# Splitting a weight load in four and reordering fillers and one AV in a fused attention and feed-forward kernel

## The chip, the cores and the metric

The kernel runs on one core of a Trainium2 chip. The metric is the device time of one execution in microseconds (us). One execution was also recorded by the hardware profiler; all times inside the execution are counted from the start of its recorded span. TensorE (PE) does the matmuls, VectorE (DVE) and ScalarE (ACT) do the elementwise work, GpSimd (POOL) does elementwise work and issues most loads, SyncE (SP) issues the rest.

## The reference

Eight batches of attention with 8 heads over 576 tokens, head size 64, are followed by a feed-forward layer over all 4608 tokens. The attention is a sum of two: one over tokens averaged by fours, whose result is repeated four times, and one in which each token sees only tokens less than four away.

```python
q_d = q.reshape(B, H, Sd, 4, D).mean(axis=3)       # k_d, v_d alike
out_up = np.repeat(sm_attn(q_d, k_d, v_d), 4, axis=2)
scores = np.where(abs(pos[:, None] - pos[None, :]) < 4, scale * q @ k.T, -1e9)
out_local = softmax(scores) @ v
x = (out_up + out_local).transpose(0, 2, 1, 3).reshape(B * S, H * D)   # 4608 x 512
h = x @ w_in                                       # 512 x 2048
out = (h * sigmoid(1.702 * h)) @ w_out             # 2048 x 512
```

## The kernel before

The order of the instructions on every engine is written out by hand (a manual schedule), so each engine executes its instructions in the order in which the code names them.

The feed-forward layer works in nine groups of 512 tokens. For one group, `mm1` (L706) multiplies 16 blocks of 128 columns of `w_in` with the transposed x (`hps_mm`, L690, matmul at L691, four steps of 128 over the 512 inputs) and `silu` (L701) writes each block to `gT`; `mm2` (L715, matmul at L747) multiplies `gT` with `w_out` into four tiles of 128 tokens, which ScalarE copies (L732) and SP stores (L737). Inside each group, at fixed positions, stand the steps of the attention of the next batch (`attention`, L648).

The first batch's attention stands ahead of all this, in its own order (L785 to L870), and it is there that the change is made. Its heads are taken in four pairs, hp 0 to 3. The steps are: the local scores (`scores`, L356, matmul at L367) and the averaged ones (`scores_d`, L378, matmul at L386); the exponentials on ScalarE (L397, L403); the averaged values by matmuls with a selection matrix (`prep_vd_pe`, L320, matmul at L329, copied by ScalarE at L338); then for each pair the local AV (`av_local0`, L500, matmul at L506) and the AV over averaged tokens, called the down AV here (`av_down0`, L514, matmuls at L520 and L529), both into one PSUM tile `o[hp]`. `normalise0` (L544) divides on VectorE: part "a" takes the columns of the local AV alone, part "b" the rest, each with a reciprocal (L548) and multiplications (L551, L556). `turned` (L848) transposes the normalised pair with matmuls (`transp_sum`, L564, matmuls at L571 and L582) and has ScalarE copy it into `xT` (`copy_x`, L590; L594 where the result lies in the two banks PM, L598 elsewhere). After the third and fourth pair, `part` (L843) starts the first group's L691 matmuls, as far as the finished pairs allow.

Between these steps stand fillers, `warm` (L641): matmuls of zeros at L644 into a PSUM bank, whose results are not read. `wz` holds zeros in bf16, `wf` in fp32. Without a named bank `warm` takes the next of the two banks PM in turn (`pm_tile`, L78).

The loads of w_in (`load_w_in`, L237), w_out (`load_w_out`, L246), k and q (`load_1`, L181) and, for the first two batches, v (`load_vb`, L214) are issued by POOL, in the order of the code. They turn fp32 in DRAM into bf16. POOL's loads use eight semaphores in turn, and each issue waits until the load eight places earlier has landed. `w_in_bf` is one tile; a matmul that reads some of its columns waits for the load that wrote those columns.

Of the kernel before, what the change touches and what calls it, by code (L numbers as in the profile page):

```python
# [19 lines left out]
def kernel(  # L20
# [48 lines left out]
    PM = [psum.tile([128, 512], FP32, name=f"pm{i}") for i in range(2)]  # L69
# [8 lines left out]
    def pm_tile():  # L78
        turn["m"] += 1
        return PM[turn["m"] % 2]  # L80

    wz = consts.tile([128, 512], BF16, name="wz")
    wf = consts.tile([128, 512], FP32, name="wf")
# [49 lines left out]
    def make_mask():  # L133
        nc.scalar.copy(
            out=mask.rearrange("p x (i c) -> p (x i) c", c=60),
            in_=dm[:, None, :].to_broadcast([128, 10, 60]),
        )
# [76 lines left out]
    def load_vb(b, i):  # L214
        for par in range(2):
            nc.gpsimd.dma_start(  # L216
                out=vbs[b % 2][64 * par : 64 * par + 64, i, :, 0:D],
                in_=bass.AP(
                    tensor=v.tensor,
                    offset=v[b, 0].offset + (114 * i + KSTART[par]) * D,  # L220
                    ap=[[D, 64], [S * D, H], [1, D]],
                ),
            )
# [13 lines left out]
    def load_w_in(c, n):  # L237
        nc.gpsimd.dma_start(
            out=w_in_bf[:, :, c : c + n],
            in_=bass.AP(  # L240
                tensor=moe_w_in.tensor, offset=moe_w_in.offset + c,
                ap=[[d_ff, 128], [128 * d_ff, n_dmc], [1, n]],
            ),
        )
# [133 lines left out]
    def scores_d(b, qd, sd=None):  # L378
        sd = sd or ps_tile()
        bank = banks(sd)  # L380
        for kc in range(3):
            for a in range(2):
                for r in range(4):
                    rows = slice(32 * r, 32 * r + 32)
                    j = r % 2
                    nc.tensor.matmul(  # L386
                        bank[r // 2][64 * j : 64 * j + 64, SD * kc : SD * kc + SD],
                        lhsT=kdT[qd][rows, 48 * kc : 48 * kc + 64, a],
                        rhs=qdT[b, qd][rows, :, a],
                        start=(a == 0), stop=(a == 1),  # L390
                        tile_position=(32 * r, 64 * j),
                    )
        return sd
# [8 lines left out]
    def exp_down(qd, sd):  # L402
        nc.scalar.activation(  # L403
            out=eds[qd][:, :, 0:432], in_=sd[:, :, 0:432],
            func=AF.Exp, scale=inv_sqrt_d / 16.0,
        )
# [107 lines left out]
    def av_down0(hp, o):  # L514
        Ed, vd, u = eds[hp // 2], vds[0], hp % 2
        h0 = hp - u
        for kc in range(3):
            for j in range(2):
                q0 = SD * kc + 128
                nc.tensor.matmul(  # L520
                    o[64:128, j, 260:390],
                    lhsT=Ed[64 * j : 64 * j + 48, u, q0 : q0 + 64],
                    rhs=vd[64 * j : 64 * j + 48, kc, h0 : h0 + 2, :],
                    start=(kc == 0), stop=(kc == 2),
                    tile_position=(64 * j, 64),
                )
        for kc in range(3):
            for j in range(2):
                nc.tensor.matmul(  # L529
                    o[:, j, 390:455],  # L530
                    lhsT=Ed[64 * j : 64 * j + 48, u, SD * kc : SD * kc + 128],
                    rhs=vd[64 * j : 64 * j + 48, kc, hp, :],
                    start=(kc == 0), stop=(kc == 2),
                    tile_position=(64 * j, 0),
                )
# [8 lines left out]
    def normalise0(o, y, u, parts="ab"):  # L544
        yl, yd, rc = y
        ov = o[:, :, 0:455].rearrange("p x (c e) -> p x c e", e=65)
        c0, c1 = {"a": (0, 4), "b": (4, 7), "ab": (0, 7)}[parts]
        nc.vector.reciprocal(rc[:, :, c0:c1], ov[:, :, c0:c1, 64:65])  # L548
        if "b" in parts:
            st = 2 - u  # L550
            nc.vector.tensor_tensor(  # L551
                out=yd.rearrange("p s x d -> p x s d"), in0=ov[:, :, 4 + u : 7 : st, 0:D],
                in1=rc[:, :, 4 + u : 7 : st].to_broadcast([128, 2, 2, D]), op=ALU.mult,
            )
            c1 = 6
        nc.vector.tensor_tensor(  # L556
            out=yl[:, :, c0:c1], in0=ov[:, :, c0:c1, 0:D],
            in1=rc[:, :, c0:c1].to_broadcast([128, 2, c1 - c0, D]), op=ALU.mult,
        )
# [4 lines left out]
    def transp_sum(y, x):  # L564
        y, yd = y[:2]
        for n, (slot, to, what) in enumerate((
            (1, x[0][:, 0:288], up(0, 72)),
            (1, x[1][:, 0:224], up(72, 128)),
            (0, x[1][:, 224:288], up(64, 80)),
        )):  # L570
            nc.tensor.matmul(  # L571
                to, lhsT=yd[:, slot, :, :], rhs=what,
                start=n < 2, stop=True, skip_group_check=True,
            )
        for m, par, pos0, n, c0, c1 in (
            (0, 0, 0, 2, 3, 60), (0, 0, 0, 1, 0, 3), (0, 1, 0, 2, 0, 57),
            (1, 0, 0, 1, 3, 60), (1, 0, 1, 1, 3, 60), (1, 1, 0, 2, 0, 57),
            (2, 0, 0, 1, 3, 60), (2, 1, 0, 1, 0, 60),
        ):
            t0 = 114 * (2 * m + pos0) + 60 * par + c0  # L580
            bank, t0 = t0 // 288, t0 % 288
            nc.tensor.matmul(  # L582
                sub(x[bank], t0, (114, n), (1, c1 - c0)),
                lhsT=y[:, par, 2 * m : 2 * m + 2, :],
                rhs=sub(id128, 64 * pos0 + c0, (64, n), (1, c1 - c0)),
                start=False, stop=True, skip_group_check=True,
            )
        return x

    def copy_x(b, hp, x):  # L590
        t0 = b * S
        if x is PM:
            for u in range(2):
                nc.scalar.copy(  # L594
                    out=xT[hp][:, t0 + 288 * u : t0 + 288 * u + 288], in_=x[u][:, 0:288]
                )
        else:
            nc.scalar.copy(  # L598
                out=xT[hp][:, t0 : t0 + S].rearrange("p (x t) -> p x t", x=2), in_=x,
            )  # L600
# [40 lines left out]
    def warm(n, cols=512, t=None, z=wz):  # L641
        t = pm_tile() if t is None else t
        for _ in range(n):
            nc.tensor.matmul(  # L644
                t[:, 0:cols], lhsT=z[:, 0:128], rhs=z[:, 0:cols], start=True, stop=True
            )
# [133 lines left out]
    o, y, x = {}, {}, {}  # L780
# [11 lines left out]
    for i in range(5):  # L792
        load_vb(0, i)
    for c in range(4):
        load_w_in(512 * c, 512)
    for qd in range(NQ):
        load_qk(1, qd)
# [19 lines left out]
    sp = scores(0, 1, barred=True, sp=PA[0:2])  # L817
    exp_local(1, sp)
    exp_down(0, scores_d(0, 0, PA[2]))
    warm(4)  # L820
    for hp in range(4):
        o[hp] = PA[hp % 3]
        y[hp] = y_tiles0()
# [9 lines left out]
        normalise0(o[hp], y[hp], hp % 2, "b")  # L833
    av_local0(2, o[2], range(5))
    normalise0(o[2], y[2], 0, "a")
    warm(2, t=PM[0], z=wf)
    make_mask()

    gT0 = new_gT()
# [8 lines left out]
    def turned(hp, n):  # L848
        x = PM if n is None else [PA[n][:, u, :] for u in range(2)]
        transp_sum(y[hp], x)  # L850
        copy_x(0, hp, PM if n is None else PA[n][:, :, 0:288])

    turned(0, None)
    av_down0(2, o[2])
    normalise0(o[2], y[2], 0, "b")
    turned(1, 1)
    av_local0(3, o[3], range(5))
# [87 lines left out]
```

## Time and profile before

| | us |
|---|---|
| median of 3 runs | 324.64 |
| lowest and highest run | 322.55, 325.23 |
| the profiled execution | 323.04 |
| its span, first to last instruction | 321.2 |
| PE busy | 312.3 (97% of the span) |
| ACT, POOL, DVE busy | 183.7, 139.3, 134.0 |

The mean granted TensorE clock of the profiled execution is 1.000. "Busy" counts the time in which an engine has at least one instruction in work. In the lists of instructions a row starts with its start and its length in us, then engine, source line and operation, then output and inputs with their shapes, the number of instructions, and in brackets the idle time ahead of it with what ended it ("issue" is idle time for which the profile shows no cause). Matmuls overlap, so the length of a group is somewhat more than the distance from its start to that of the next. PEld is TensorE's loading of weights.

### The profile page before, as it was taken

What the parts mean: (1) busy time and instruction counts of PE and PEld (TensorE: products, weight loads), DVE (VectorE), ACT (ScalarE), POOL (GpSimd) and SP (SyncE); (2) the same over time, 40 slices, a digit from 0 to 9 for tenths busy, and PEclk for the clock granted to TensorE, in tenths of its full rate; (3) what the DMA queues carried; (4) which work ended last, traced back from release to release, by engine and by line L of the source; (5) the groups of instructions that cost most, each with busy time, mean ns of one, the idle gap of its engine ahead of it and who ended that gap; (6) DMA issues with size and microseconds to landing.
All of it is one profiled execution on the core that took longest, in us unless ns stands there. A gap on an engine that the chain in (4) does not pass through costs nothing.

```text
span 321.2 us, 10997 instructions
## 1 busy us (share of the span) xinstructions
PE 312.3 (97%) x4927; PEld 157.6 (49%) x4927; DVE 134.0 (42%) x221; ACT 183.7 (57%) x314; POOL 139.3 (43%) x170
## 2 busy tenths in 40 slices
PE   6899999999999989999999999999999999999995
PEld 3565554445544445455545554555445544444444
DVE  6965326812773066605770478036811650000000
ACT  4465771767456663668365936583677466415611
POOL 8956950299009910794059604970296000000000
PEclk9999999999999999999999999999999999999999
DMA  7999999999519931796159815991360110020012
GB/s 121 128 206 207 170 149 216 183 248 209 132 68 198 201 97 67 168 215 147 66 147 205 177 40 147 200 203 49 109 106 2 70 67 2 0 98 33 2 62 68
DMA packets 64078, 40.02 MB, mean 125 GB/s; under 512 B 44064, under 2 KB 55456, under 8 KB 64032
## 3 DMA queue, kind: packets, MB, share of 16 engines
q1 hardware_dynamic: 44496, 24.32, 33.0%
q0 software_dynamic: 19392, 14.95, 31.9%
q8 instruction: 38, 0.62, 0.8%
q10 hardware_dynamic: 144, 0.07, 0.1%
q14 instruction: 8, 0.07, 0.1%
HBM read 44.83 MB, written 9.44 MB: 169 GB/s over the span
## 4 chain that ended last, share of the span: by engine, by line
PE 94%; DVE 2%; DMA 2%; issue 1%; POOL 0%; ACT 0%; POOLq 0%
PE pm L691 37%; PE pm L747 37%; PE pa L367 3%; PE pa L747 2%; PE pa L691 2%; PE pa L428 2%; PE pa L386 2%; PE pa L481 2%; DMA qb<-in_q_dram 2%; PE pa L450 2%; PE pm L762 1%; PE pm L644 1%; DVE qT L262 1%; PE pa L491 0%; PE pa L506 0%
## 5 line engine op out<-in xcount | busy, mean ns | idle before, releaser
L747 PE MATMUL pm<-w_out_bf,gT 128*128 128x512 bf16 x528 | 121.8, 380 | 0.3 <-issue 0.3
L691 PE MATMUL pm<-xT,w_in_bf 128*128 128x512 bf16 x544 | 121.1, 379 | 0.0
L702 ACT ACTIVATE gT<-pm 128x512 bf16<-128x512 f32 x136 | 81.0, 598 | 44.6 <-PE pm L691 44.6
L691 PEld LDWEIGHTS <-w_in_bf 128*128 128x128 bf16 x576 | 55.5, 98 | 66.9 <-issue 0.4
L747 PEld LDWEIGHTS <-gT 128*128 128x128 bf16 x560 | 51.4, 98 | 59.8 <-issue 1.0
L411 DVE TENSOR_TENSOR es<-es,mask 128x600 bf16<-128x600 bf16 x28 | 20.0, 730 | 88.8 <-ACT es L397 88.0
L292 POOL TENSOR_TENSOR pq<-kT 128x576 f32<-128x576 bf16 x14 | 16.2, 1159 | 90.0 <-DVE kT L262 90.0
L732 ACT ACTIVATE osb<-pm 128x512 f32<-128x512 f32 (+2 forms) x35 | 20.8, 594 | 40.4 <-PE pm L747 36.5
L605 ACT COPY od<-pa 128x384 f32<-128x384 f32 (+1 forms) x56 | 18.5, 412 | 32.2 <-DVE y L467 19.7
L467 DVE TENSOR_TENSOR y<-pa,rc 128x896 bf16<-128x896 f32 x28 | 30.6, 1092 | 1.0
L626 DVE TENSOR_TENSOR xT<-pa,od 128x570 bf16<-128x570 f32 x28 | 21.1, 753 | 11.4 <-ACT od L605 10.1
L734 DVE TENSOR_SCALAR osb<-pm 128x128 f32<-128x128 f32 x1 | 0.3, 292 | 55.3 <-ACT osb L732 55.3
L308 POOL TENSOR_TENSOR v<-v 112x512 f32<-112x512 f32 x18 | 22.8, 1266 | 0.0
L397 ACT ACTIVATE es<-pa 128x600 bf16<-128x600 f32 x32 | 19.7, 668 | 5.2 <-PE pa L367 5.0
L262 DVE STREAM_TRANSPOSE kT<-kb 128x576 f32<-128x576 f32 x16 | 20.0, 1249 | 3.5 <-DMA kb<-in_k_dram 3.4
L262 DVE STREAM_TRANSPOSE qT<-qb 128x576 f32<-128x576 f32 x16 | 19.9, 1241 | 0.4
L367 PEld LDWEIGHTS <-kT 32*64 32x64 bf16 x1280 | 11.7, 104 | 8.5 <-issue 6.4
L367 PE MATMUL pa<-qT,kT 32*64 32x60 bf16 x1280 | 13.6, 203 | 1.9 <-DVE qT L262 1.9
L216 POOL DMA_DIRECT2D vb<-in_v_dram x20 | 13.7, 698 | 3.0 <-DMA w_in_bf<-in_moe_w_in_dram 1.1
L292 POOL TENSOR_TENSOR pq<-qT 128x576 f32<-128x576 bf16 x13 | 14.9, 1146 | 0.0
L403 ACT ACTIVATE ed<-pa 128x864 bf16<-128x864 f32 x16 | 14.4, 898 | 0.1
L311 POOL TENSOR_TENSOR vd<-v 112x256 bf16<-112x256 f32 x18 | 13.7, 759 | 1.4
(92 smaller groups left out, 257.9 us busy)
## 6 DMA issues: line engine op xcount, KB each, us to landing
out_dram<-osb SPq DMA_DIRECT2D x35, 256.0 KB, 2.1
vf<-in_v_dram SPq DMA_DIRECT2D x60, 128.0 KB, 5.3
v<-in_v_dram SPq DMA_DIRECT2D x36, 192.0 KB, 5.1
kb<-in_k_dram POOLq DMA_DIRECT2D x16, 288.0 KB, 7.2
qb<-in_q_dram POOLq DMA_DIRECT2D x16, 288.0 KB, 8.3
w_in_bf<-in_moe_w_in_dram POOLq DMA_DIRECT2D x4, 512.0 KB, 9.1
w_out_bf<-in_moe_w_out_dram POOLq DMA_DIRECT2D x4, 512.0 KB, 12.6
vb<-in_v_dram POOLq DMA_DIRECT2D x20, 64.0 KB, 5.4
```

The source lines that it names most:

```text
L262: nc.vector.transpose(out=t32.rearrange("p (i c) -> p c i", c=18), in_=store[b, qd].bitcast(FP32).rearrange("p (c d) -> p c d", c=18),)
L292: nc.gpsimd.tensor_tensor(out=t1, in0=sv[:, :, 0:2, :], in1=sv[:, :, 2:4, :], op=ALU.add)
L308: eng.tensor_tensor(out=t1[0:112], in0=x[:, :, 0:2, :], in1=x[:, :, 2:4, :], op=ALU.add)
L367: nc.tensor.matmul(sp[r // 2][64 * par : 64 * par + 64, r % 2, 60 * i : 60 * i + 60], lhsT=kT[b, qd][rows, k0 : k0 + 64, a], rhs=qT[b, qd] ...
L397: nc.scalar.activation(out=es[2 * qd + u][:, :, 0:300], in_=sp[u][:, :, 0:300], func=AF.Exp, scale=inv_sqrt_d,)
L411: nc.vector.tensor_tensor(out=ev, in0=ev, in1=mask, op=ALU.mult)
L467: nc.vector.tensor_tensor(out=y[:, xs], in0=ov[:, :, :, 0:D], in1=rc[:, xs].to_broadcast([128, n, 7, D]), op=ALU.mult,)
L626: eng.tensor_tensor(out=sub(xT[hp], t0 + 3, (57, 2), (114, 5), (1, 57)), in0=sub(x, 3, (509, 2), (57, 5), (1, 57)), in1=sub(od, 3, (57, 2) ...
L691: nc.tensor.matmul(acc, lhsT=w_in_bf[:, dmc, ffc * 128 : (ffc + 1) * 128], rhs=xT[dmc][:, g * TG : g * TG + TG], start=(dmc == 0), stop=(d ...
L702: nc.scalar.activation(out=gT[:, ffc, :], in_=acc, func=AF.Silu, scale=GELU_SCALE)
L732: eng.activation(out=osb, in_=ap, func=AF.Copy, scale=1.0 / GELU_SCALE)
L747: nc.tensor.matmul(ops[t], lhsT=gT[:, ffc, t * 128 : (t + 1) * 128], rhs=w_out_bf[:, ffc, :], start=(ffc == 0), stop=(ffc == n_ffc - 1),)
```

## The change

Three places of the first batch's order change. The first 512 columns of w_in are loaded by four transfers of 128 columns each, in place of one of 512; the other three transfers of 512 follow as they did. The four bf16 fillers ahead of the averaged values become one fp32 filler into the bank PM[1], named instead of taken in turn, and of the two fp32 fillers behind the third pair's local AV one stays. The third pair's down AV is called ahead of the first `turned` instead of behind it; its normalisation "b" stays behind that `turned`.

```diff
@@ -792,6 +792,8 @@
     for i in range(5):
         load_vb(0, i)
     for c in range(4):
+        load_w_in(128 * c, 128)
+    for c in range(1, 4):
         load_w_in(512 * c, 512)
     for qd in range(NQ):
         load_qk(1, qd)
@@ -817,7 +819,7 @@
     sp = scores(0, 1, barred=True, sp=PA[0:2])
     exp_local(1, sp)
     exp_down(0, scores_d(0, 0, PA[2]))
-    warm(4)
+    warm(1, t=PM[1], z=wf)
     for hp in range(4):
         o[hp] = PA[hp % 3]
         y[hp] = y_tiles0()
@@ -833,7 +835,7 @@
         normalise0(o[hp], y[hp], hp % 2, "b")
     av_local0(2, o[2], range(5))
     normalise0(o[2], y[2], 0, "a")
-    warm(2, t=PM[0], z=wf)
+    warm(1, t=PM[0], z=wf)
     make_mask()
 
     gT0 = new_gT()
@@ -850,8 +852,8 @@
         transp_sum(y[hp], x)
         copy_x(0, hp, PM if n is None else PA[n][:, :, 0:288])
 
+    av_down0(2, o[2])
     turned(0, None)
-    av_down0(2, o[2])
     normalise0(o[2], y[2], 0, "b")
     turned(1, 1)
     av_local0(3, o[3], range(5))
```

## The prediction

> **What bounds the kernel.** I read the page's chain of work first, then TensorE's (PE) instructions in order of time from 13 to 30 us, where all three edits lie, then VectorE's (DVE) in the same stretch, and last the DMA issues with their times to landing.
>
> ```profile
> span 321.2 us, 10997 instructions
> ...
> PE   6899999999999989999999999999999999999995
> ...
> PE 94%; DVE 2%; DMA 2%; issue 1%; POOL 0%; ACT 0%; POOLq 0%
> ```
>
> TensorE carries 94% of the chain that ended last, and is full in nearly all slices. A microsecond is won only if TensorE gets to its dense matmuls (L691, L747) earlier, and nothing late stops it after that. The stretch that the change edits, in order of time (start, length, engine, line):
>
> ```profile
> 14.07 1.02 PE L644 MATMUL pm<-wz 128*128 128x512 bf16 x4 [0.31 <-issue]
> 15.03 0.83 PE L329 MATMUL pm<-vb,psel 128*64 128x256 bf16 x10
> ...
> 18.21 0.36 PE L520 MATMUL pa<-vd,ed 48*64 48x130 bf16 x6 [0.28 <-DVE yl L556]
> 18.50 0.27 PE L529 MATMUL pa<-vd,ed 48*128 48x65 bf16 x6
> 18.70 0.38 PE L506 MATMUL pa<-vb,es 64*64 64x65 bf16 x20
> 19.00 2.28 PE L644 MATMUL pm<-wf 128*128 128x512 f32 x4
> 21.12 0.41 PE L571 MATMUL pm<-id,yd 128*128 128x288 bf16 x3
> ...
> 21.75 0.36 PE L520 MATMUL pa<-vd,ed 48*64 48x130 bf16 x6
> ...
> 22.24 0.42 PE L571 MATMUL pa<-id,yd 128*128 128x288 bf16 x3
> ...
> 22.88 0.34 PE L506 MATMUL pa<-vb,es 64*64 64x65 bf16 x18
> ```
>
> The reader is to see that TensorE has no hole between 14 and 23 us longer than 0.31 us, but that the two L644 rows are fillers: their result is read by nobody. The two fp32 fillers (four passes, 19.00 to 21.12) cover a wait on VectorE:
>
> ```profile
> 19.86 0.20 DVE L548 RECIPROCAL rc<-pa 128x8 f32<-128x8 f32 x1
> 20.09 0.69 DVE L556 TENSOR_TENSOR yl<-pa,rc 128x512 bf16<-128x512 f32 x1
> ```
>
> This is the third pair's local normalisation. It reads the same accumulator that the pair's down AV (L520, L529) writes, and the order of instructions has that AV wait for VectorE. The price of such a release stands in the second pair: its L556 ran from 17.47 for 0.70 in the chain, to 18.17, and L520 started at 18.21, 0.04 later. The last two lines are landing times, in us after the issue: the first block of w_in (issued at 12.98) and the last block of the second batch's values (issued at 39.98).
>
> ```profile
> w_in_bf<-in_moe_w_in_dram POOLq DMA_DIRECT2D x1, 512.0 KB, 5.9
> vb<-in_v_dram POOLq DMA_DIRECT2D x1, 64.0 KB, 4.4
> ```
>
> **Part 1: four bf16 fillers become one fp32 filler.** Before, L329 starts 0.96 after the first bf16 filler (14.07 to 15.03). One fp32 filler is two passes. In the later pair of them the passes start at 19.00, 19.54, 20.27 and 20.70, and L571 follows at 21.12: so one filler takes 1.27 (19.00 to 20.27) or 0.85 (20.27 to 21.12). Against 0.96 that is -0.11 to +0.31. The 0.31 of issue ahead of the old filler may stay or go, so L329 could start up to 0.42 sooner or 0.31 later. Neither passes through whole: the last two of the first ten L329 loads sat idle 0.16 until 15.55 for the eighth value transfer (issued 10.71, landed 4.8 later, 15.51). Sooner gains at most 0.04; later loses 0.31 - 0.16 = 0.15. I take 0, as the two lengths lie 0.1 apart at the nearer row. Everything up to the local AV of the third pair (18.70) then stands where it was.
>
> **Parts 2 and 3: one of the two later fillers goes, and the third pair's down AV moves ahead of the first transposition.** They have one answer together. The local AV of pair 2 ends its starts at 19.00; one filler runs to 20.13 (second pass 19.54 + 0.59), at most 20.27. The next instruction is now the down AV's first matmul, which waits for the L556 that ends at 20.78. VectorE is not sped up by anything here: its work since 16.39 is released by the AVs ahead of the filler. So TensorE stands from 20.13 to 20.82 (20.78 + 0.04). Behind the waiting matmul stand, in TensorE's order, the first transposition (L571, L582), and with it ScalarE's copy of x (L594) that was 1.46 us idle anyway. From 20.82: down AV 0.49 (21.75 to 22.24), first transposition 0.63 (21.12 to 21.75), second 0.64 (22.24 to 22.88): 22.58. Before, the same point is 22.88. Gain 0.30. The same from the other side: 1.27 or 0.85 of filler leaves, and 0.69 of bare wait comes in its place. VectorE's end at 20.78 fixes this; I allow 0.1 either way for the start gaps.
>
> What comes next keeps its distance. Copies of x by ScalarE: the first transposition now ends near 22.0, the copy takes 0.70, and its first reader stands at 23.51 - 0.30 = 23.21. Pair 2's second normalisation starts about 21.35 instead of 22.35, and is needed near 23.4 instead of 23.74. Pair 3 moves as a whole. The filler names its PSUM bank instead of taking a turn, so the banks of all later tiles swap: mm2 of group 0 now first writes the bank that the last silu reads. That silu ends at 39.21 (38.61 + 0.60) and L747 starts at 39.66: 0.45 cover, and both move together. Cost 0; without the cover it would be the missing part of 0.45.
>
> **Part 4: w_in's first 512 columns in four transfers.** On TensorE nothing is won: the first block landed at 18.88 and its first reader started at 23.51. On POOL three more issues at 0.78 are 2.35 us. They delay the issues of the second batch's k and q, w_out and values; POOL idled for landings right after (1.03 and 2.34 ahead of w_out, 1.06 ahead of a value load), and up to there the queue holds several transfers, so the issue time itself costs 0. Each of those issues still waits for the transfer eight places earlier, which past the new ones is the same transfer as before.
>
> What can cost is the stream. The 512 packets of 1024 bytes become 2048 of 256. Rows of large packets moved 208 GB/s (18 to 20 us): 2.5 us for 512 KB. Rows of 128-byte packets moved 2135 packets in 2 us (10 to 12 us). At that packet rate 2048 packets take 1.9 us, a gain of 0.6; at that stretch's bytes (141 GB/s) 3.7 us, a loss of 1.2; at its worst stretch (96 GB/s, 12 to 14 us) 5.5 us, a loss of 2.9. 256 bytes lie nearer 128 than 1024, and a line through 0.94 ns a packet at 128 bytes and 4.9 at 1024 gives 1.5 ns, so 3.1 us: I take 0.6 later. Who meets it? The least cover is at the second batch's values: the last landed at 39.98 + 4.4 = 44.4, and L329 reads them at 46.49, or 46.19 after the gain: 1.8 us. w_out's first blocks landed at 35.8 and 38.35 for readers at 39.66 and 41.4; w_in's second at 22.0 for a reader past 26.7; the second batch's k and q, for which VectorE idles until 28.59, are read by TensorE at 38.50. SP's queue is not moved past: its first load waits for w_out's last block, at 50.45. A delay of 0.6 costs 0; 2.9 would cost 2.9 - 1.8 = 1.1.
>
> The Trainium skill speaks against this part: "DMA: Bandwidth & Descriptors", Specifications, wants at least 512 bytes a transfer, and says that below that the engine reads, modifies and writes. If that doubles the 2.5 us, the estimate by that page is 2.5 us later and 0.7 us lost, where the packet rows above make it nothing; the 128-byte rows here (141 GB/s against 208) do not show a doubling.
>
> **Sum.** 0 - 0.30 + 0 = -0.30; ends -0.44 (0.04 and 0.1 more gained) and +1.05 (-0.30 + 0.1 + 0.15 + 1.1). The profiled execution took 323.04 us (span 321.2), so 322.74. The median of the runs is 324.64, 1.60 above it, and the runs spread from 322.55 to 325.23; against the median I say 324.3.
>
> **Rivals.** *Nothing moves:* 0.3 us is given back at an issue gap downstream, as the 0.34 at L747 near 56.1 in the waits. For it: such gaps stand still while work moves. Against it: they need no common cause. 324.6.
>
> *The clock.* Less filler, and 0.69 of bare wait, could let TensorE slow down. The profile's granted clock is 1.00 throughout, but the first fillers (128x336) start 0.28 apart until about 5 us and 0.14 after, so half speed exists here, and left some 3.8 us after the first filler. Half speed for 3.8 us of the dense stretch costs 1.9. Against: TensorE stood 1.92 us with no matmul (6.74 to 8.66), and the ten fillers after that took 2.33, 0.22 a piece, full speed. It decides from a standstill of more than 1.9 us, or from too little work in the same few us. The price is 1.9 - 0.3 = 1.6: 326.2; two such stretches would be 328.1.
>
> The Trainium skill ("TensorE: Matmul & The Clock Gate", Why this matters for your kernels) allows idle gaps up to about 3 us. By it the clock holds and the sum stays; the 1.92 row agrees as far as it reaches.
>
> *The stream is late.* If w_in's pieces cost over 1.8 us, L329 at 46.49 stops for the values. At the worst row it ends at 324.64 - 0.3 + 1.1 = 325.4. This is slower than before, from one place.
>
> *More is won.* The runs' spread of 2.7 us means that some executions hold a wait which this profile doesn't show. If that is a late first block of w_in, four pieces give it back: up to the 1.6 between the median and the profiled execution, 324.64 - 0.3 - 1.6 = 322.7. Against it: 4.6 us of cover in the profile.
>
> **How the numbers follow.** Forecast 0.55, nothing moves 0.13, clock 0.14, late stream 0.10, more won 0.08. The predicted time is 324.3. The low end, 322.4, is the more-won case with 0.3 for its tail; the high end, 326.3, is the clock case; both leave under 2 in 10, with the runs' spread inside. The likeliest case's own range is 323.8 to 325.4. About 1% (3.2 us) is what a measurement of this kernel can tell from no change. Over 1% faster needs twice the more-won case: 0.04. Over 1% slower needs two slow clock stretches, or the clock and the stream together: 0.10. Within 1%: 0.86.
>
> **What would show it.** Right: one f32 filler from about 14.0 and one from 19.0; a TensorE hole ending near 20.8, released by L556; L520 then, L571 near 21.3, the second L571 near 21.9, the first L691 at 23.2; w_in's fourth piece landing 18.5 to 20; L329 at 46.2 without a DMA wait. Wrong: no hole there (the AV didn't wait), L691 at 0.43 a piece (the clock), a DMA wait at L329 or L747 between 39 and 50 us, or the first L691 no earlier than 23.5.

## The result and the profile after

| | us |
|---|---|
| changed kernel, median (21 runs) | 325.91 (323.74 to 328.18) |
| kernel before, median of its 21 runs beside them | 324.45 (322.55 to 325.73) |
| ratio of the two, 95% interval | 1.0054 [1.0033, 1.0075] |
| profiled execution after, and its span | 327.87, 326.1 |

The change costs 0.5%, about 1.7 us by the ratio and 1.5 by the medians (the ratio is not the quotient of the two medians). The interval leaves out no change, and so the forecast's 0.3 us of gain: the sign was wrong. From the page after: the span, the packets of POOL's loads (q0: packets, MB, share of 16 engines' time), and the chain by engine.

```profile
span 326.1 us, 10992 instructions
...
q0 software_dynamic: 20976, 14.95, 33.8%
...
PE 91%; DMA 4%; issue 2%; POOL 1%; DVE 1%; ACT 0%; POOLq 0%
```

The same row of the page before:

```profile
q0 software_dynamic: 19392, 14.95, 31.9%
```

TensorE (PE) lost 3 points of the chain, and waits for DMA and "issue" took them. The bytes are the same; 1584 packets came on top (1536 by the split, and 16 more for each of three more transfers), and the packets took a larger share of a longer span. TensorE's instructions after, where the edits lie (start, length, line, and the idle time ahead with what ended it):

```profile
14.06 1.02 PE L644 MATMUL pm<-wf 128*128 128x512 f32 x2 [0.22 <-issue]
15.01 0.64 PE L329 MATMUL pm<-vb,psel 128*64 128x256 bf16 x8
16.23 0.31 PE L329 MATMUL pm<-vb,psel 128*64 128x256 bf16 x2 [0.58 <-DMA vb<-in_v_dram]
16.47 0.47 PE L506 MATMUL pa<-vb,es 64*64 64x65 bf16 x17
17.24 0.41 PE L506 MATMUL pa<-vb,es 64*64 64x65 bf16 x23 [0.31 <-DMA vb<-in_v_dram]
...
19.89 0.38 PE L506 MATMUL pa<-vb,es 64*64 64x65 bf16 x20
20.20 1.12 PE L644 MATMUL pm<-wf 128*128 128x512 f32 x2
22.03 0.36 PE L520 MATMUL pa<-vd,ed 48*64 48x130 bf16 x6 [0.70 <-DVE yl L556]
...
23.69 0.35 PE L506 MATMUL pa<-vb,es 64*64 64x65 bf16 x18
```

Read it in three pieces. Up to 15.01 nothing moved (15.03 before). Then matmuls wait twice for the first batch's values, 0.58 and 0.31, which the trace of before does not have; with the shorter holes around them they make the third pair's local AV start at 19.89 instead of 18.70, 1.19 later. From there to the fourth pair's local AV it is 23.69 - 19.89 = 3.80, where it was 22.88 - 18.70 = 4.18: 0.38 won, with the bare wait for L556 as forecast. In all the first L691 starts at 24.33, 0.82 later than before.

The transfer that carries the last of those values is the last one issued ahead of the pieces. Its row after (issue to landing, last column):

```profile
vb<-in_v_dram POOLq DMA_DIRECT2D x1, 64.0 KB, 4.8
```

It was issued at about 12.4 and landed at 17.20; before, the same transfer took 3.7 us and landed at 16.00. Ahead of it the queue is the same in both kernels, behind it stand the pieces; that these held it up is likely by this pair of traces, but not shown by it (a second profile of the changed kernel, e16 below, has 3.4 us). The other 4.1 us of this execution's 4.9 lie behind 24 us. TensorE's waits after, by line (total, times, longest, us):

```profile
PE pa L450 <- issue: 3.6, 3, 1.4
...
PE pa L520 <- DVE yl L556: 1.0, 2, 0.7
...
PE pa L481 <- issue: 0.8, 1, 0.8
PE pm L329 <- DMA vb<-in_v_dram: 0.6, 1, 0.6
```

Nearly all is "issue": in the chain, six such gaps behind 24 us add up to 5.2 us, and to 1.6 in the trace of before (four gaps). What they are, the counts show. TensorE's matmuls (third column) and weight loads (fourth) from the start to the gap near 57 us, before and then after:

```profile
0.00:56.30 56.30, 52.09 (x991) 28.70 (x991) 33.70 (x70) 30.69 (x50) 36.54 (x60) 1.00 1.31 171
```

```profile
0.00:58.90 58.90, 53.38 (x991) 29.31 (x991) 35.00 (x72) 31.12 (x50) 38.78 (x63) 1.00 1.37 161
```

991 + 991 = 1982 instructions in both, though the change takes eight away ahead of it and the place in the code is another. Counted in the same way inside the other gaps, 447, 1726, 2749, 3005 and 4028 instructions have started: each step is a multiple of 256, to one instruction. The page also lists a queue of kind "instruction" with 38 packets and 0.62 MB, 16 KB each, and 38 blocks of 256 are 9728 of TensorE's 9846 instructions. In the 18 profiles of this document TensorE has 75 issue gaps over 0.2 us, and each ended 1.2 to 1.9 us after a packet of that queue was done, though such packets come some 8 us apart. So the gaps are the borders of blocks of 256 instructions, where TensorE waits for the next block. The Trainium skill ("Runtime: NRT & Kernel Launch", Instruction fetch mechanics) describes such blocks of 16 KiB, fetched by a DMA queue of the engine's own, and calls the cost of a border mostly hidden. The runs here agree with the blocks; the cost is hidden in most of them, and 0.2 to 1.7 us at a few. How long a gap is differs between executions of one kernel, so a single pair of profiles (4.9 us apart, where the medians are 1.5 apart) overstates the change. The question for the runs is which edit carries the 0.5%.

### The profile page after: what moved, and what is told of

The parts are those of the page before. It is cut to its first block, busy times and chain, and to the rows that moved or that the text cites. A ratio compares the mean times of both kernels' runs of the same rounds, so it can differ in the third digit from the quotient of the medians.

```text
span 326.1 us, 10992 instructions
## 1 busy us (share of the span) xinstructions
PE 313.1 (96%) x4923; PEld 158.4 (49%) x4923; DVE 134.1 (41%) x221; ACT 183.7 (56%) x314; POOL 141.6 (43%) x173
## 4 chain that ended last, share of the span: by engine, by line
PE 91%; DMA 4%; issue 2%; POOL 1%; DVE 1%; ACT 0%; POOLq 0%
PE pm L691 36%; PE pm L747 36%; PE pa L367 3%; PE pa L747 2%; DMA qb<-in_q_dram 2%; PE pa L691 2%; PE pa L428 2%; PE pa L481 2%; PE pa L386 2%; PE pa L450 2%; DMA vb<-in_v_dram 1%; PE pm L762 1%; DVE yl L556 1%; PE pa L491 1%; POOL vb L216 0%
## 5 line engine op out<-in xcount | busy, mean ns | idle before, releaser
L747 PE MATMUL pm<-w_out_bf,gT 128*128 128x512 bf16 x528 | 121.7, 380 | 0.0
L691 PE MATMUL pm<-xT,w_in_bf 128*128 128x512 bf16 x544 | 121.1, 379 | 0.0
L691 PEld LDWEIGHTS <-w_in_bf 128*128 128x128 bf16 x576 | 55.6, 98 | 66.8 <-issue 0.4
L747 PEld LDWEIGHTS <-gT 128*128 128x128 bf16 x560 | 51.6, 98 | 59.1 <-issue 0.2
L367 PEld LDWEIGHTS <-kT 32*64 32x64 bf16 x1280 | 11.8, 104 | 7.5 <-issue 6.2
L466 DVE RECIPROCAL rc<-pa 128x14 f32<-128x14 f32 x28 | 6.7, 241 | 20.5 <-PE pa L450 20.3
L367 PE MATMUL pa<-qT,kT 32*64 32x60 bf16 x1280 | 13.6, 203 | 0.9 <-DVE qT L262 0.9
```

Source lines behind the costliest of these rows:

```text
L367: nc.tensor.matmul(sp[r // 2][64 * par : 64 * par + 64, r % 2, 60 * i : 60 * i + 60], lhsT=kT[b, qd][rows, k0 : k0 + 64, a], rhs=qT[b, qd] ...
L691: nc.tensor.matmul(acc, lhsT=w_in_bf[:, dmc, ffc * 128 : (ffc + 1) * 128], rhs=xT[dmc][:, g * TG : g * TG + TG], start=(dmc == 0), stop=(d ...
L747: nc.tensor.matmul(ops[t], lhsT=gT[:, ffc, t * 128 : (t + 1) * 128], rhs=w_out_bf[:, ffc, :], start=(ffc == 0), stop=(ffc == n_ffc - 1),)
```

## The experiments

The theory to begin with: the split of w_in (Part 4) costs, and Parts 1 to 3 do not. The rivals: the fillers or the moved AV cost; eight instructions fewer put the borders of the blocks in worse places. Each kernel was timed beside the kernel before, whose medians were 324.07 us beside e1 to e4, 323.47 beside e5 to e8, 324.25 beside e9 to e12 and 323.44 beside e13 to e16; intervals are 95%.

**e1, the changed kernel without the split.**

```diff
-        load_w_in(128 * c, 128)
-    for c in range(1, 4):
         load_w_in(512 * c, 512)
```

> The changed kernel with the first 512 columns of w_in in one transfer again; fillers and the moved AV stay as changed. Stream theory (the four pieces make the load stream late, and later loads then collide with TensorE's fetches of instructions): the loss goes, ratio to the kernel before 0.999 (-0.3 us), second w_in block lands 1.5 to 3 us earlier than in the changed kernel. Position theory (8 TensorE instructions fewer move the borders of the 256-instruction blocks to worse places): the loss stays, ratio 1.005, TensorE issue gaps 4 to 5 us in the profile. Front theory (the wait ahead of the moved AV itself costs): 1.005.

Measured: 324.5 us, 1.0006 [0.998, 1.0031]. The loss can no longer be told. The front is as forecast, the hole with its length (TensorE in order of time, e1):

```profile
15.73 0.88 PE L506 MATMUL pa<-vb,es 64*64 64x65 bf16 x40
...
20.98 0.36 PE L520 MATMUL pa<-vd,ed 48*64 48x130 bf16 x6 [0.70 <-DVE yl L556]
```

No wait for values at L506, and 3.79 us from the third to the fourth pair's local AV. The interval holds -0.3 us (0.9991) and no change alike.

**e2, the kernel before with the split alone.**

```diff
     for c in range(4):
+        load_w_in(128 * c, 128)
+    for c in range(1, 4):
         load_w_in(512 * c, 512)
```

> The kernel before with only w_in's first 512 columns in four transfers. Stream theory: ratio 1.005, issue gaps of TensorE over 3 us in the profile. Position theory: ratio 1.000, issue gaps near 1.5 us as in the kernel before. Front theory: 1.000.

Measured: 325.33 us, 1.003 [1.0009, 1.0051]. The loss is there without the other edits, and so is a part of the wait:

```profile
16.66 0.41 PE L506 MATMUL pa<-vb,es 64*64 64x65 bf16 x23 [0.28 <-DMA vb<-in_v_dram]
```

**e3 and e4, the position of the blocks.** Other fillers at the very start give the changed kernel its eight instructions back, and take eight from the kernel before; the filler work stays nearly the same.

```diff
-    warm(21, 336)
+    warm(25, 282)    # e3, in the changed kernel
+    warm(17, 415)    # e4, in the kernel before
```

> The changed kernel whose first filler run is 25 matmuls of 282 columns in place of 21 of 336: the same columns in all, but 8 instructions more on TensorE, so that behind the fillers every instruction stands where it stood in the kernel before. Position theory: the loss goes, ratio 0.999. Stream theory: the loss stays, 1.005. Front theory: 1.005.

> The kernel before whose first filler run is 17 matmuls of 415 columns in place of 21 of 336: the same columns, 8 instructions fewer on TensorE, so that behind the fillers every instruction stands where it stands in the changed kernel. Position theory: ratio 1.005 to 1.006 and issue gaps over 3 us. Stream and front theory: ratio 1.000.

Measured: e3 325.27 us, 1.0037 [1.0009, 1.0065]; e4 324.03 us, 1.0009 [0.9985, 1.0034]. The loss stays with the split, wherever the borders lie. So the position is not the cause.

Next: is it the neighbourhood of the values in the queue? **e5 splits the last 512 columns instead of the first**, 1.5 MB behind the values, in the kernel before.

```diff
-    for c in range(4):
+    for c in range(3):
         load_w_in(512 * c, 512)
+    for c in range(12, 16):
+        load_w_in(128 * c, 128)
```

> The kernel before with the last 512 columns of w_in in four transfers of 128 instead of the first 512: as many issues and small packets, but behind three large transfers. Neighbour theory (small packets queued right behind the first batch's values make the last value transfers land later, and TensorE waits for them at L329 and L506): last value transfer lands 3.5 to 3.7 us after its issue, no wait at L506, ratio 1.000. Stream theory (all that follows lands later and meets TensorE's instruction fetches): ratio 1.003 to 1.005.

Measured: 324.38 us, 1.0036 [1.0016, 1.0055]. The last values landed 3.8 us after their issue and nothing waited for them,

```profile
15.80 0.78 PE L506 MATMUL pa<-vb,es 64*64 64x65 bf16 x40
```

and yet the loss is the same. So the wait at the values cannot be all of it.

**e6 cuts the first 512 columns in eight**: packets of 128 bytes.

```diff
-    for c in range(4):
+    for c in range(8):
+        load_w_in(64 * c, 64)
+    for c in range(1, 4):
```

> The kernel before with the first 512 columns in eight transfers of 64: the suspected cost doubled. Stream theory: 4 more issues of 0.75 us and 128-byte packets, the second w_in block lands about 3 us later than with four pieces, readers of the second batch's values and of w_out begin to wait, ratio 1.008 or more. Neighbour theory: the last value transfer lands 4.1 to 4.8 us after its issue, as with four pieces, and the ratio stays at 1.003 to 1.005 unless a later reader waits.

Measured: 326.31 us, 1.0085 [1.0055, 1.0115]: more than twice the mean loss of the kernels with four pieces (table below). Its profile shows a DMA wait that a later stream would bring, at the first `mm2`:

```profile
PE pm L747 <- DMA w_out_bf<-in_moe_w_out_dram: 1.2, 2, 0.9
```

A smaller one stands there in e1 too, which loses nothing:

```profile
PE pm L747 <- DMA w_out_bf<-in_moe_w_out_dram: 0.3, 1, 0.3
```

**e7 and e8, the other two ideas alone**, in the kernel before. e7 has both filler edits; e8 drops both later fillers and transposes the first two pairs ahead of the third pair's down AV, so that real work covers L556.

```diff
-    warm(4)                              # e7
+    warm(1, t=PM[1], z=wf)               # e7
...
-    warm(2, t=PM[0], z=wf)               # e7 and e8
+    warm(1, t=PM[0], z=wf)               # e7
...
     turned(0, None)
+    turned(1, 1)                         # e8
     av_down0(2, o[2])
     normalise0(o[2], y[2], 0, "b")
-    turned(1, 1)                         # e8
```

> The kernel before with the two filler edits alone: no split, the third pair's down AV behind the first transposition as before. By the times of the kernel before: first transposition 20.13 to 20.76, down AV released by VectorE at 20.82, second transposition ends 21.95 instead of 22.88: -0.9 us, ratio 0.997. If less filler slows TensorE: L691 more than 0.22 us apart, ratio above 1.003. If what is won there is lost again downstream: 1.000.

> The kernel before without the later filler pair, and with the first two transpositions both ahead of the third pair's down AV, so that they fill the wait for VectorE: down AV released near 20.8, local AV of the fourth pair from 21.3 instead of 22.9: -1.5 us, ratio 0.995. If the gain is lost again, because the second batch's values then arrive too late for L329 (cover 1.8 us less 1.2): waits on them at L329, ratio 0.997 to 1.000. If the clock falls: above 1.003.

Measured: e7 322.89 us, 0.9988 [0.997, 1.0005]; e8 323.07 us, 0.9982 [0.9958, 1.0007]. Both lean the expected way by less than expected (0.4 and 0.6 us instead of 0.9 and 1.5), and neither is told apart from no change. In both profiles a block border took some of what was won, e7 and e8:

```profile
21.33 0.19 PE L571 MATMUL pm<-id,yd 128*128 128x64 bf16 x1 [0.85 <-issue]
```

```profile
20.52 0.19 PE L571 MATMUL pm<-id,yd 128*128 128x64 bf16 x1 [0.67 <-issue]
```

That this comes of a faster TensorE isn't shown: e13 below keeps all fillers and has a gap of 0.83 at the same border. e8 lost something else as well: in 5 of its 12 executions the mean granted clock was 0.995 or less (last section).

Three more rivals for the split: the three added issues themselves, POOL's time for them (2.35 us), and POOL's late k and q sums. **e9 cuts the first 512 columns in four by rows** (128 rows of w_in each: three more issues, but packets of 1024 bytes as before); **e10 adds 2.65 us of memset on POOL** behind the first w_in transfer; **e11 and e12 hand a sum of k from POOL to VectorE**, in e8 and in the changed kernel.

```diff
+    for d in range(4):
+        load_w_in_rows(d, 512)           # e9: w_in_bf[:, d, 0:n], 128 rows
...
+    load_w_in(0, 512)                    # e10
+    nc.gpsimd.memset(v4[32:64], 0.0)     # e10
-    for c in range(4):
+    for c in range(1, 4):                # e9, e10
         load_w_in(512 * c, 512)
...
-            pool_qk(1, 1, "k")
+            reduce_qk(1, 1, "k")         # e11, e12
```

> The kernel before with the first 512 columns of w_in in four transfers by rows of w_in (128 rows, all 512 columns each): three more issues as in the change, but packets of 1024 bytes as before. Packet theory (the 256-byte packets make the loads late): ratio 1.000. Issue theory (three more issues on POOL push back all that POOL issues behind them): if an issue of 128 packets costs 0.56 us as those of k and q, POOL is 1.5 us later, ratio 1.002 to 1.003.

> The kernel before, w_in in four transfers of 512 as before, with 2.65 us of other work on POOL (the memset of a later buffer, done twice) between the first and the second of them: POOL's time of the three issues without their transfers. Issue theory: ratio 1.003 to 1.004, second batch's last value transfer issued 2 us later. Packet theory: 1.000.

> No split, no later fillers, first two transpositions ahead of the third pair's down AV, and one sum over k of the second batch moved from POOL (1.17 + 0.66 us) to VectorE, which idles there (one reduction of 1.35 us from 35.4). Late-load theory: POOL's issues behind it come 1.8 us earlier, and the 1.5 us won at the front are kept: ratio 0.995. If loads behind POOL do not matter: 0.998 as without it.

> The changed kernel with the same sum moved from POOL to VectorE. Late-load theory (the loss is in what POOL issues late after 38 us): most of the loss goes, ratio 1.000 to 1.002. Neighbour theory (the loss is in the first batch's values, before 18 us): it stays, 1.004.

Measured: e9 324.54 us, 0.9987 [0.9959, 1.0014]; e10 325.02 us, 1.0009 [0.9979, 1.0039]; e11 323.94 us, 0.9982 [0.9949, 1.0015]; e12 325.6 us, 1.0045 [1.0016, 1.0074]. Four transfers cost nothing that can be told while their packets stay large, and with them falls most of POOL's time: from the first to the last of e9's w_in issues POOL took 1.55 us more than before (2.2 more in e2), and e9's interval ends at 0.14%. e10 alone would not settle it, as its interval reaches 0.39%. Freeing POOL of the sum does not take the loss away. What remains of the split is its small packets.

The last four test that: **e13 halves** (two of 256 columns, packets of 512 bytes), **e14 puts the pieces behind the second 512 columns**, **e15 is the kernel before again** and **e16 the changed kernel again**, both without an edit.

```diff
-    for c in range(4):
+    for c in range(2):                   # e13
+        load_w_in(256 * c, 256)          # e13
+    for c in range(1, 4):                # e13
...
+    load_w_in(512, 512)                  # e14
+    for c in range(4):                   # e14
+        load_w_in(128 * c, 128)          # e14
+    for c in range(2, 4):                # e14
         load_w_in(512 * c, 512)
```

> The kernel before with the first 512 columns of w_in in two transfers of 256 columns: packets of 512 bytes, half as many as in the change, one more issue. If the loss belongs to packets under 512 bytes: ratio 1.000. If it goes by the number of packets: a third of the change's extra 1536, that is 512 more, and a third of the loss, 1.001.

> The kernel before with the first 512 columns in four transfers of 128, issued behind the second 512 columns, so that one large transfer lies between the values and the small packets. Neighbour theory: the last value transfer lands 3.5 to 3.8 us after its issue again, no wait at L506, ratio 1.000. Packet theory (small packets cost wherever they stand): 1.003 to 1.004, as with the last 512 columns split. If the first reader of w_in has to wait instead: a DMA wait at L691 near 23.5.

> The kernel before once more, unchanged, as one of the kernels to be compared: shows how far a ratio strays by itself. All theories: 1.000, interval about 0.003 to either side. Its profile gives a second execution: landing of the last value transfer 3.5 to 4.2 us after its issue by the packet theories.

> The changed kernel once more. Ratio 1.004 to 1.006. Second profile: last value transfer 4.1 to 4.8 us after its issue, waits for it at L329 or L506; if executions differ by a fall of the clock as in the run without later fillers, a granted clock of 0.5 somewhere between 18 and 28 us in some of them.

Measured: e13 323.68 us, 1.0006 [0.9979, 1.0033]; e14 323.93 us, 1.002 [1.0001, 1.004]; e15 323.28 us, 0.9995 [0.997, 1.0021]; e16 324.75 us, 1.0032 [1.0011, 1.0054]. Packets of 512 bytes lose nothing that can be told, pieces behind a large block still lose, and the change repeats. e16's profile has no wait for the first batch's values, and the kernel is slower all the same. The last two of them, issue to landing:

```profile
vb<-in_v_dram POOLq DMA_DIRECT2D x2, 64.0 KB, 3.4
```

All together, by the size of the packets of the split block:

| packets | added | kernels | ratio to before |
|---|---|---|---|
| 512 bytes or more | up to 512 | e1, e4, e7 to e11, e13, e15 | 0.9982 to 1.0009, each interval holds 1 |
| 256 bytes | 1536 | changed, e2, e3, e5, e12, e14, e16 | 1.0020 to 1.0054, mean 1.0036, each interval above 1 (the changed kernel and e16 are the same program) |
| 128 bytes | 3584 | e6 | 1.0085 |

The mean of 0.36% is 1.2 us of 324, over 1536 packets 0.8 ns a packet; e6's 0.85% is 2.7 us, over 3584 packets 0.8 ns as well. The 512 added packets of e13 would be 0.4 us by that, 0.12%, which its interval holds. So whether the loss begins under 512 bytes or grows with the number of packets from the first isn't told apart.

## Why the prediction failed, step by step

**Part 1: right.** Taken at 0. The one filler took 0.95 (14.06 to 15.01), between the two lengths that were weighed, and L329 starts at 15.01 after and at 15.03 before.

**Parts 2 and 3: right, in mechanism and about in size.** The hole was forecast from the end of the filler to L556 + 0.04; it is there in the changed kernel and in e1, 0.70 long and released by L556. The gain between the two local AVs is 0.38 and 0.39 where 0.30 was forecast. In the time it can't be seen: e1 is at 1.0006, with an interval that holds the gain and also none of it. The swap of the banks that was priced at 0 is in e1 and e7 too, which lose nothing that can be told.

**Part 4: "A delay of 0.6 costs 0" is the step that failed.** The term of the sum was 0, with 1.1 us as its bound; the split measured +1.0 us alone (e2), and 1.2 as the mean of the seven measurements with 256 bytes. The delay itself was about right for the pieces: in the five profiles with four pieces right behind the values, the second 512 columns landed 7.5 us after the last values on the mean, in the ten without small packets 6.7. That is 0.8 where 0.6 was forecast, though the two ranges overlap (7.0 to 8.1 and 5.4 to 7.2). What was wrong is "costs 0", and two things in the way to it.

First, the step asked only who reads what is issued *behind* the pieces. The last values of the first batch, issued just *ahead* of them, landed 4.1 to 4.9 us after their issue in five of the six profiles with small pieces right behind them (after, e2, e3, e6, e12; 3.4 in e16), and 3.5 to 4.2 in the others; in the kernels with four pieces there they landed 0.75 us later on the mean (16.87 against 16.12 without small packets). Their cover in the trace of before is short: they landed at 16.00, and L506 was reading values from 15.79. Matmuls that wait for the first batch's values, 0.15 to 0.9 us in all, stand in four profiles (after, e2, e12, e14), all with packets of 256 bytes, and in none with larger ones. (Weight loads of L329 wait for values in most profiles, in that of before too, for 0.42 and 0.16; under a filler or earlier matmuls that costs little.) e14's wait of 0.15 has a whole block between the values and the pieces, so it need not come of them. These waits aren't the whole cause: e3, e5 and e16 lose without them.

Second, the cover behind was taken from one execution. At the second batch's values it was 2.1 us before (landed 44.35, read at 46.49) and 0.4 after (landed 46.87, read at 47.31): nearly spent, without a wait, in that profile. But in e15, the same kernel as before, they landed at 45.87 and were read at 46.73, a cover of 0.9 without any split. Such a cover moves by more than the 0.6 us that was to be hidden in it, so it may be gone in some executions; for these values no profile shows that. What a spent cover costs, e6 shows with its w_out: 1.2 us at L747.

**The page's rule was nearer than the row.** The Trainium skill ("DMA: Bandwidth & Descriptors", Specifications) asks for at least 512 bytes a transfer; the prediction's estimate by it was a loss of 0.7 us. That this lies near the 1.0 to 1.2 measured is partly luck: it was put at a wait of L329 for the second batch's values, which no profile shows. The runs agree with the place of the page's threshold, without singling it out: 256 and 128 bytes lose, 512 and 1024 do not by more than their intervals allow. They don't show the mechanism it names.

**The rivals.** The late stream (325.4, at a chance of 0.10) came nearest, but not by its own place: L329 did not wait at the second batch's values in the changed kernel. The clock is not the cause: the granted clock of the changed kernel's two profiles is 1.000 and 0.999 on the mean. In 4 of its 21 executions it was 0.995 or less, and these took 326.9 to 328.2 us; the median of the other 17 is 325.61. The kernels e2, e6, e14 and e16 had no such execution and are slower all the same. "Nothing moves" named the issue gaps; they are real, and they blur every profile here, but their position did not cause the loss (e3, e4).

**What stays open.** Through which wait the small packets cost in executions like e3's, e5's and e16's isn't settled. A stream that lands later and blocks of instructions that are fetched later would both fit a cost that grows with the number of packets; one profile of each kernel can't separate them: the issue gaps over 0.15 us behind 24 us add up to 1.6 in before and 2.5 in e15, the same kernel, and to 5.2 in after and 2.8 in e16, the same kernel. On the mean of the profiles the first L691 starts 0.3 us later with small packets (8 profiles, 23.8 us) than without (10 profiles, 23.5), and what follows it takes 1.0 us longer (299.5 against 298.5); with single ones from 297.3 to 301.8 this only hints that most is paid behind 24 us. So what is shown is that the small packets carry the loss, and that more of them lose more; not where it is paid.

No version clearly beats the kernel before. e7 and e8 come nearest, both with intervals that still hold 1.

## What to carry to other kernels

Cutting a load into more transfers cost nothing that could be told here while each row stayed at 512 bytes or more: cut by rows (e9) or in halves (e13), not into narrow columns. When a load gets slower, look at the transfers queued ahead of it as well as at those behind, and take a cover from several executions: 2.1 us in one profile was 0.9 in another of the same kernel. A sum of 0.3 us cannot be confirmed on a kernel whose executions of one program spread over 3 us.

## What the runs showed of the hardware

The fetch of instructions can stop TensorE in a stretch of many small matmuls. It was longest in e11, where 1.69 us of it fell inside the first transposition, behind the third pair's local AV (TensorE in order of time, e11):

```profile
21.35 0.21 PE L571 MATMUL pm<-id,yd 128*128 128x64 bf16 x1 [1.69 <-issue]
```

What followed stands in the granted clock, third column from the right of the busy times by stretch (e11):

```profile
19.00:20.00 1.00, 0.66 (x24) 0.43 (x23) 0.97 (x4) 0.99 (x2) 0.00 (x0) 1.00 1.23 211
20.00:21.00 1.00, 0.00 (x0) 0.00 (x0) 0.96 (x3) 0.52 (x1) 0.00 (x0) 0.84 1.25 203
21.00:24.00 3.00, 2.65 (x51) 2.17 (x54) 0.19 (x2) 1.34 (x3) 0.97 (x2) 0.50 1.24 208
24.00:27.00 3.00, 2.78 (x46) 1.76 (x36) 2.34 (x6) 0.21 (x1) 2.96 (x2) 0.50 1.23 210
27.00:28.00 1.00, 1.00 (x5) 0.47 (x4) 0.00 (x0) 0.43 (x1) 0.43 (x2) 0.75 1.13 209
28.00:29.00 1.00, 1.00 (x15) 0.71 (x13) 0.00 (x0) 0.38 (x1) 0.48 (x1) 1.00 1.12 210
```

The clock fell to a half about 1 us into the gap and stayed there past 27 us, into the dense matmuls. In that execution the second batch's first scores (L367) started at 41.03 instead of 37.71 in e8, 3.3 us later; 1.0 of that is the longer gap (0.67 in e8). The standstill of 1.92 us in the trace of before, behind dense fillers, did not lower the clock (the ten fillers after it started 0.22 apart); this shorter one, amid sparse small matmuls, did. So of the two conditions of the prediction's clock rival, the first (a standstill of more than 1.9 us) was drawn too wide, and the second (too little work in the same few us) is nearer to what e11 shows. The Trainium skill ("TensorE: Matmul & The Clock Gate", Why this matters for your kernels), which the prediction weighed, allows gaps up to about 3 us; 1.69 was enough here, and the measurement decides.

The mean granted clock of an execution tells whether it fell anywhere. It was 0.995 or less in 6 of 12 executions of e11 and 5 of 12 of e8, the two kernels without the later fillers, and in 27 of 317 of the others, those of the kernel before beside e1 to e16 included. e11's six took 325.0 us on the mean, its other six 323.3. So the rival was right to fear for the clock where both later fillers go (these two kernels also transpose a pair earlier, which wasn't tested apart). Where one of the two stays, as in the changed kernel, it does not show: 8 of 81 executions, against 19 of 236 where both stay. What was won in e8 and e11 was partly lost again in this way.
